# Turned keys placed four copies to a block in the next unit's feed-forward, and unit 7's keys turned on VectorE too

## The chip, the cores and the metric

The kernel runs on one core of a Trainium2 chip. The core has five engines that run side by side, each from its own queue in order: TensorE (matrix products; PE in the profile, PEld for its weight loads), VectorE (DVE), ScalarE (ACT), GpSimd (POOL) and SyncE (SP, which here only issues DMA transfers). The metric is the time of one execution in microseconds (us); the runs of one kernel are told by their median.

## The reference

Two parts follow each other. The first is a linear attention with a complex decay, for 4 batches, 8 heads, 768 tokens and a head width of 48; the second a feed-forward layer on its output, without a nonlinearity between the two products.

```python
scale = np.minimum(mag, 0.999) / (mag + 1e-06)          # mag = |a_re + i a_im|
for t in range(S):                                      # S = 768, D = 48
    S_re, S_im = ar * S_re - ai * S_im + kv, ar * S_im + ai * S_re
    y[:, :, t] = np.einsum('bhd,bhde->bhe', q[:, :, t], S_re)
x = y.transpose(0, 2, 1, 3).reshape(B * S, H * D)       # 3072 x 384
return (x @ w_a) * (x @ w_b) @ w_out                    # d_ff = 1536
```

## The kernel before

**Units.** The work is cut into 12 units (`NU`): two pairs of batches, and for each pair six chunks of 128 tokens of all heads. A unit is 256 tokens of the feed-forward. Within a chunk the recurrence is written as matrix products: decays are multiplied up along the chunk (*preparation*, `prep`), queries and keys are scaled by them, and then come scores, outputs and the update of the carried state (*attention*, `attn`).

**Stages.** The main loop runs over `w`, the unit whose feed-forward is worked. I call one turn of it stage w. It has 12 blocks `f`, one for each 128 of the 1536 hidden columns. In a block TensorE makes the first product (`gemm1`, L546, 18 products into a PSUM bank `ab`, of which there are three), and then the second product (`gemm2`, L567, 6 products into the two output banks `o`) of the block two before (`LAG = 2`), so the last two second products of a unit run in blocks 0 and 1 of the next stage. Then the output banks are evicted by two copies on ScalarE (L706) before block 2's second product, the first of the new unit, may write them; there is one pair of banks.

Behind each first product stands a chain: ScalarE copies half the bank (L557, into `h_t` or, in odd blocks, into a buffer `o_sb`), VectorE multiplies by the other half (L558), ScalarE rounds to `hh` (L559), VectorE makes the rest `hl` (L560). The second product reads `hh` and `hl`.

**Attention between the blocks.** In stage w the attention of unit w+1 is laid piece by piece between the products: scores (L429, masked by VectorE into `am`, L432), transposes of the keys, outputs (L473), rest of the outputs, state (L496, which reads the turned keys `kt`). `ATTN_AT` or `LATE_ATTN_AT` says in which block it begins; it is over by block 10 or 11 (`STACK_AT`). The preparation of unit w+2 also runs on VectorE and ScalarE in stage w and the end of the one before; its results go out as ten or so transfers `stk<-qk` on SyncE (`stack`, L366).

**Turning the keys.** The state product needs the keys with tokens on the partitions. Up to unit 7 (`KT_FROM = 8`) TensorE turns them: 16 transposes for a unit (L440), evicted by four copies on ScalarE (L443). From unit 8 on `turn_keys` turns 32x32 blocks on VectorE (four instructions, L396) into the unit's own decay tile `a_t`, and `place_keys` puts the blocks in their place in `kt` with 16 copies on ScalarE (L406). There is one buffer `kt`. These 16 copies are issued in one go in block 10 of the stage before the one whose attention reads them. A unit without a next chunk (5 and 11) needs no turned keys.

What hangs on `KT_FROM` besides: in a unit turned on VectorE the two products of queries and keys with the decays (L319, 1536 elements wide) are cut into four of 768, attention begins in block 4 (`LATE_ATTN_AT`) and has 13 pieces for 16; and the load of the decay tile of unit u+2 is put off, since the turned keys lie in the old one (`apool` has two buffers). `late_decays` (units from `KT_FROM + 2`) says that a unit's decay scaling (`scale`, five passes on VectorE and seven on ScalarE) is made at the start of its own preparation and not within the one before.

**Order.** A scheduler orders each engine's instructions by priority and by dependences, after costs of its own; `tc.high_priority` lifts the chain behind the first product and the attention's evictions, and `tc.issue_after(x)` keeps an instruction behind x on the queue. `ff_last[0]` is the last matrix product of the feed-forward.

Of the kernel before, what the change touches and what calls it, by code (L numbers as in the profile page):

```python
# [22 lines left out]
NU = NBP * NCH  # L23
# [22 lines left out]
LAG = 2  # L46
HB = 3
OWN_FROM = 2
KT_FROM = 8
GATE_FROM = 2  # L50
O_BUFS = 3
CONV_ON_AB = 7
# [20 lines left out]
def tile_kernel(ctx: ExitStack, tc: tile.TileContext, a_d, qk_d, v_d, w_d, qn_d, kn_d, vn_d, an_d, out_d):  # L73
    nc = tc.nc
    vec, act, pe, sync = nc.vector, nc.scalar, nc.tensor, nc.sync
# [48 lines left out]
    def r(ap):  # L124
        return ap.bitcast(F32R)
# [34 lines left out]
    def load_a(u):  # L160
        t = apool.tile([128, 2, W], F32, name="a_t")
        for hs in halves if u == 0 else (slice(0, W),):
            sync.dma_start(out=t[:, :, hs], in_=a_d[u, :, :, hs])
        return t

    a_tiles = {}
# [38 lines left out]
    def late_decays(u):  # L205
        return u >= KT_FROM + 2 and (u - 1) % NCH

    def prep(u):
# [129 lines left out]
        yield 1000  # L338
        if u < KT_FROM or c + 1 == NCH:
            for k in range(2):  # L340
# [14 lines left out]
    def load_qk(u):  # L355
        sync.dma_start(out=qk[:, :, 1, 0:2 * TOK], in_=qk_d[u])

    def stack(u):
        n = RUN if rescaled(u % NCH) else 2 * TOK
        for h in range(H):  # L360
            r0 = h * D
            while r0 < (h + 1) * D:
                j, p = divmod(r0, 128)
                m = min((h + 1) * D - r0, 128 - p)
                d0 = 2 * (r0 - h * D)
                sync.dma_start(out=stk[d0:d0 + 2 * m, h, 0:n], in_=qk[p:p + m, j, :, 0:n])  # L366
                r0 += m
# [4 lines left out]
    def load_v(u):  # L372
        for i in range(2):
            t = vpool.tile([128, VW], F32, name="v_t")
            for c0, s0, n in ((0, 0, 64), (64, 80, 48)):
                sync.dma_start(out=t.rearrange("p (g e) -> p g e", g=H // 2)[:, :, c0:c0 + n],
                               in_=v_d[u, i].rearrange("p (g e) -> p g e", g=H // 2)[:, :, s0:s0 + n])
            v_tiles[u, i] = t
# [9 lines left out]
    kt_pending = {}  # L388

    def new_kt(u):  # L390
        kt_tiles[u] = kvp.tile([128, 2, H * KS], F32, name="kt", bufs=1)
# [8 lines left out]
    def place_keys(u, t):  # L400
        new_kt(u)
        src = t.rearrange("p s w -> p (s w)").rearrange("p (t g x) -> p t g x", t=4, g=G)
        dst = kt_tiles[u].rearrange("p i (j b x) -> p (i j) b x", j=NJ, b=4)
        for tb in range(4):
            for pb in range(4):
                act.copy(out=dst[tb * 32:(tb + 1) * 32, :, pb], in_=src[pb * 32:(pb + 1) * 32, tb])  # L406

    ff_last = [None]

    def attn(u, xh, xl):  # L410

# [2 lines left out]
        ams, xps = {}, {}  # L414
        if not last and u < KT_FROM:
            new_kt(u)
# [71 lines left out]
        def state(i, hg):  # L488
# [12 lines left out]
            with tc.high_priority(offset=ATTN_FIRST):  # L501
# [4 lines left out]
                if rescaled(c):  # L506
# [5 lines left out]
                 (state, 1, 0), (residual, 1, 0), (state, 1, 1)]  # L512
        if u >= KT_FROM:
            order = [(scores, 0, 0), (scores, 0, 1), (pause, 0, 0), (outputs, 0, 0), (scores, 1, 0),
# [7 lines left out]
        for fn, i, g in order:  # L522
            if not (last and fn is state or fn is transposes and (last or u >= KT_FROM)):
                fn(i, g)
                yield

    def pieces(u):
        if u >= KT_FROM:
            return 9 if u % NCH + 1 == NCH else 13
        return 8 if u % NCH + 1 == NCH else 16  # L530

    def new_x():
        return (moe.tile([128, NJ, TOK], F32, name="xh"), moe.tile([128, NJ, TOK], F32, name="xl"))


    def w_ab(f, part, blk):
        m, b = divmod(blk, NJ)
        return w_t[f, m][:, part, b * 128:(b + 1) * 128]

    def gemm1(f, xh, xl, ps_ab=ps_ab, moe=moe, spare=None):  # L540
        ab = ps_ab.tile([128, 512], F32, name="ab")
        for m in range(2):
            n = 0
            for i in range(NJ):
                for part, xt in ((0, xh), (0, xl), (1, xh)):
                    ff_last[0] = pe.matmul(out=ab[:, m * TOK:(m + 1) * TOK],  # L546
                              lhsT=r(w_ab(f, part, m * NJ + i)),
                              rhs=r(xt[:, i, :]), start=n == 0, stop=n == 8).ins
                    n += 1
        if spare and f % 2:  # L550
            h_t = spare()[:, 0:TOK]
        else:
            h_t = moe.tile([128, TOK], F32, name="h_t", bufs=1)
        hh = moe.tile([128, TOK], F32, name="hh", bufs=HB)
        hl = moe.tile([128, TOK], F32, name="hl", bufs=HB)
        with tc.high_priority(offset=MOE_FIRST):
            act.copy(out=h_t, in_=ab[:, 0:TOK])  # L557
            vec.tensor_tensor(out=h_t, in0=ab[:, TOK:2 * TOK], in1=h_t, op=ALU.mult)  # L558
            act.copy(out=r(hh), in_=h_t)  # L559
            vec.tensor_tensor(out=r(hl), in0=h_t, in1=hh, op=ALU.subtract)  # L560
        return hh, hl

# [113 lines left out]
    def drain(gen, ns=None):  # L676
        if gen is None:
            return
        left = ns
        for cost in gen:  # L680
            if left is not None:
                left -= cost or 0
                if left <= 0:
                    return
# [14 lines left out]
    def second():  # L699
        w2, f2, hh, hl, os2 = pend.pop(0)  # L700
        gemm2(f2, hh, hl, os2)
        if f2 == NF - 1:
            for tt in range(2):
                o_sb = moe.tile([128, DM], F32, name="o_sb", bufs=O_BUFS)
                with tc.high_priority(offset=MOE_FIRST):
                    act.copy(out=o_sb, in_=os2[tt][:, 0:DM])  # L706
                act.dma_start(out=out_d[w2, tt], in_=o_sb)

    def spare_h(w, f):
        if w > 0:  # L710
            return lambda: moe.tile([128, DM], F32, name="o_sb", bufs=O_BUFS)
        if f <= ATTN_AT[0]:
            return lambda: kvp.tile([128, 2, H * KS], F32, name="kt", bufs=1)[:, 0]

    def attn_at(w):
        return LATE_ATTN_AT if w + 1 >= KT_FROM else ATTN_AT[min(w, 4)]

    pgen = None
    for w in range(NU):
        last = w + 1 == NU  # L720
        x_nxt = None if last else new_x()
        at = None if last else attn(w + 1, *x_nxt)
        if not last:
            load_v(w + 1)
        os_ = [ps_o.tile([128, 512], F32, name=f"o{t}") for t in range(2)]
        slots = [0, 2 * (STACK_AT[min(w, 4)] + 1 - max(attn_at(w), 0 if w else P1_AT + 1))]
        left = [pieces(w + 1)]

        def slot():
            if at is None or f < attn_at(w) or (w == 0 and f <= P1_AT) or not slots[1]:  # L730
                return
            n = -(-left[0] // slots[1])
            slots[1] -= 1
            for _ in range(n):
                next(at, None)
                left[0] -= 1

        for f in range(NF):
            if w == 0:
                next(ws, None)  # L740
                drain(p1, P1_F)
                if f == P1_AT:
                    drain(p1)
                    stack(1)
                    load_qk(2)
                    pgen = prep(2)
            pend.append((w, f, *gemm1(f, *x_cur, spare=spare_h(w, f)), os_))
            slot()
            if len(pend) > LAG:
                second()  # L750
            slot()
            if f == STACK_AT[min(w, 4)]:
                drain(at)
                if w + 2 < NU:
                    drain(pgen)
                    if w + 2 in kt_pending:
                        place_keys(w + 2, kt_pending.pop(w + 2))
                    stack(w + 2)
                if w + 3 < NU:
                    load_qk(w + 3)  # L760
                    pgen = prep(w + 3)
                if w + 4 < NU and w + 4 not in a_tiles:
                    a_tiles[w + 4] = load_a(w + 4)
            if w > 0:
                drain(pgen, 2400)
        x_cur = x_nxt
# [74 lines left out]
```

## Time and profile before

| | |
|---|---|
| median of 3 runs | 689.01 us (688.86 to 690.12) |
| profiled execution | 689.64 us, of which 687.9 is the span of the instructions |
| TensorE busy (PE) | 642.6 us, 93% |
| VectorE busy (DVE) | 555.0 us, 81% |
| ScalarE busy (ACT) | 329.1 us, 48% |
| L440, transposes of keys on TensorE | x112, 255 ns mean |
| L406, copies that place turned keys | x48, 511 ns mean |
| L706, evictions of the output banks | x22, 481 ns mean |

Times of a row are counted from the start of the span. A matrix product's duration contains the filling and draining of the array, so that of products in a row the distance from start to start is what each costs. Starts of the stages (first L546 product): stage 5 at 343.11, 6 at 393.11, 7 at 444.09, 8 at 493.25, 9 at 543.94, 10 at 594.51.

### The profile page before, as it was taken

The page shows a single profiled execution, that of the slowest core. Times are in us where ns is not written, and L with a number is a line of the kernel's source. Part 1 is how long each engine was busy: PE and PEld are TensorE (multiplying, and loading weights), DVE is VectorE, ACT ScalarE, POOL GpSimd, SP SyncE. Part 2 cuts the span into 40 slices and gives each one's busy share as a digit, 9 for nine tenths or more (in the row PEclk, how much of TensorE's full clock was granted, in tenths as well). Part 3 has the DMA queues.
Part 4 walks back from the last instruction along what each step waited for, and adds up shares of the span by engine and source line. Part 5 has one row for each costly group of instructions (what it writes and reads, how often), then busy time and mean ns, then how long its engine had stood idle before and what let it go on. Part 6 is the DMA issues. An engine that isn't in the chain of part 4 may idle for free.

```text
span 687.9 us, 14250 instructions
## 1 busy us (share of the span) xinstructions
PE 642.6 (93%) x5794; PEld 605.8 (88%) x5794; DVE 555.0 (81%) x1277; ACT 329.1 (48%) x658; POOL 5.5 (1%) x11
## 2 busy tenths in 40 slices
PE   3547899999999999999999999999999999999996
PEld 1224789999999999999999999999989989999996
DVE  5999999998989989989899899898898588432221
ACT  6347665634545446264363554555735733222221
POOL 3000000000000000000000000000000000000000
PEclk9566999999999999999999999999999999999998
DMA  8983300512415215042160340530520500400000
GB/s 286 390 312 92 118 2 7 181 51 65 122 39 150 60 51 171 16 131 92 27 192 17 108 127 2 126 109 11 157 70 18 150 24 15 106 24 2 24 1 28
DMA packets 52120, 63.14 MB, mean 92 GB/s; under 512 B 28624, under 2 KB 32208, under 8 KB 52048
## 3 DMA queue, kind: packets, MB, share of 16 engines
q1 hardware_dynamic: 48592, 57.45, 28.0%
q10 hardware_dynamic: 3456, 4.72, 1.9%
q8 instruction: 47, 0.77, 0.5%
q14 instruction: 25, 0.20, 0.1%
HBM read 38.54 MB, written 4.72 MB: 63 GB/s over the span
## 4 chain that ended last, share of the span: by engine, by line
PE 57%; DVE 26%; ACT 7%; DMA 6%; issue 2%; SPq 1%; DVEq 0%; ACTq 0%
PE ab L546 28%; PE o L567 14%; DMA w<-in_dram 5%; PE xp L473 4%; PE pm L429 4%; PE pm L496 3%; DVE a_t L299 3%; DVE qk L319 2%; ACT kt L406 2%; DVE hl L560 2%; DVE pr L237 2%; DVE z L304 1%; PE pm L440 1%; DVE am L432 1%; DVE h_t L558 1%
## 5 line engine op out<-in xcount | busy, mean ns | idle before, releaser
L546 PE MATMUL ab<-xh,w 128*128 128x256 f32 x1728 | 339.4, 285 | 0.0
L546 PEld LDWEIGHTS ab<-xh,w 128*128 128x128 f32 x1728 | 276.2, 189 | 2.4 <-issue 1.6
L546 PE MATMUL ab<-xl,w 128*128 128x256 f32 x864 | 244.3, 283 | 0.0
L546 PEld LDWEIGHTS ab<-xl,w 128*128 128x128 f32 x864 | 162.8, 188 | 0.5
L567 PE MATMUL o<-w,hh 128*128 128x384 f32 x576 | 154.0, 346 | 2.8 <-ACT o_sb L706 2.8
L567 PEld LDWEIGHTS o<-w,hh 128*128 128x128 f32 x576 | 97.1, 188 | 5.2 <-ACT o_sb L706 4.1
L567 PE MATMUL o<-w,hl 128*128 128x384 f32 x288 | 97.3, 338 | 0.0
L557 ACT COPY h_t<-ab 128x256 f32<-128x256 f32 x75 | 27.7, 370 | 72.0 <-PE ab L546 68.9
L152 PE MATMUL ab<-o_sb,ident 128*128 128x384 f32 x42 | 29.2, 794 | 30.4 <-DVE o_sb L143 30.4
L558 DVE TENSOR_TENSOR h_t<-ab,h_t 128x256 f32<-128x256 f32 x75 | 31.5, 420 | 30.7 <-ACT h_t L557 30.7
L429 PE MATMUL pm<-stk 128*128 128x128 f32 x384 | 54.8, 282 | 0.6 <-DMA stk<-qk 0.5
L429 PEld LDWEIGHTS pm<-stk 128*128 128x128 f32 x384 | 50.3, 195 | 4.7 <-issue 3.2
L567 PEld LDWEIGHTS o<-w,hl 128*128 128x128 f32 x288 | 54.1, 188 | 0.0
L557 ACT COPY o_sb<-ab 128x256 f32<-128x256 f32 x66 | 24.3, 368 | 60.5 <-PE ab L546 60.2
L559 ACT CAST hh<-h_t 128x256 fp32r<-128x256 f32 x75 | 30.1, 402 | 47.5 <-DVE h_t L558 47.3
L558 DVE TENSOR_TENSOR o_sb<-ab,o_sb 128x256 f32<-128x256 f32 x66 | 27.6, 419 | 29.0 <-ACT o_sb L557 29.0
L237 DVE TENSOR_TENSOR pr<-z 128x384 f32<-128x384 f32 (+1 forms) x91 | 47.2, 524 | 2.4 <-ACT z L223 0.3
L559 ACT CAST hh<-o_sb 128x256 fp32r<-128x256 f32 x66 | 26.6, 404 | 46.4 <-DVE o_sb L558 46.3
L152 PEld LDWEIGHTS ab<-o_sb,ident 128*128 128x128 f32 x42 | 10.2, 286 | 40.0 <-DVE o_sb L143 29.4
L299 DVE TENSOR_TENSOR a_t<-z,b_t 128x768 f32<-128x768 f32 x48 | 44.6, 951 | 0.0
L319 DVE TENSOR_TENSOR qk<-qk,z 128x768 f32<-128x768 f32 (+1 forms) x32 | 43.2, 1349 | 0.2
L560 DVE TENSOR_TENSOR hl<-h_t,hh 128x256 fp32r<-128x256 f32 x75 | 31.4, 419 | 10.5 <-ACT hh L559 10.5
(117 smaller groups left out, 898.4 us busy)
## 6 DMA issues: line engine op xcount, KB each, us to landing
w<-in_dram SPq DMA_DIRECT2D x36, 384.0 KB, 7.9
qk<-in_dram SPq DMA_DIRECT2D x12, 768.0 KB, 4.9
stk<-qk SPq DMA_DIRECT2D x48, 192.0 KB, 3.3
a_t<-in_dram SPq DMA_DIRECT2D x11, 768.0 KB, 4.3
stk<-qk SPq DMA_DIRECT2D x24, 192.8 KB, 3.4
out_dram<-o_sb ACTq DMA_DIRECT2D x24, 192.0 KB, 1.9
v_t<-in_dram SPq DMA_DIRECT2D x24, 128.0 KB, 2.7
v_t<-in_dram SPq DMA_DIRECT2D x24, 96.0 KB, 3.0
```

The lines of the kernel that those rows point to most:

```text
L152: pe.matmul(out=lp[:, 0:n], lhsT=ident, rhs=t, start=True, stop=False)
L237: vec.tensor_tensor(out=pr[:, :, :, o:o + n], in0=view(zz, W + at_(i) + 2 * o, [[W, 2], [-W, 2], [2, n]]), in1=tok(slice(1, 3), i - 1, o, ...
L299: vec.tensor_tensor(out=pz[:, s].rearrange("p (j b e) -> p j b e", j=SUB // 2, e=2), in0=zb[:, 1 + s], in1=view(bb, (1 + k - s) * NB, [[0, ...
L319: vec.tensor_tensor(out=qk4[:, :, k, x0:x1], in0=qk4[:, :, 1, x0:x1], in1=z[:, k].rearrange("p (j t) -> p j t", j=NJ).unsqueeze(2).broadca ...
L429: pe.matmul(out=sp[:, h4], lhsT=stk[:, h, ks], rhs=stk[:, h, qs], start=True, stop=True)
L473: run = pe.matmul(out=xp[qd * 32:(qd + 1) * 32, ti], lhsT=l, rhs=rr, start=st, stop=sp_, tile_position=(0, qd * 32), skip_group_check=True ...
L546: ff_last[0] = pe.matmul(out=ab[:, m * TOK:(m + 1) * TOK], lhsT=r(w_ab(f, part, m * NJ + i)), rhs=r(xt[:, i, :]), start=n == 0, stop=n == ...
L557: act.copy(out=h_t, in_=ab[:, 0:TOK])
L558: vec.tensor_tensor(out=h_t, in0=ab[:, TOK:2 * TOK], in1=h_t, op=ALU.mult)
L559: act.copy(out=r(hh), in_=h_t)
L560: vec.tensor_tensor(out=r(hl), in0=h_t, in1=hh, op=ALU.subtract)
L567: ff_last[0] = pe.matmul(out=os_[tt][:, 0:DM], lhsT=r(ht[:, ts]), rhs=r(w_t[f, 2][:, part, :]), start=(f == 0 and n == 0), stop=(f == NF - ...
```

## The change

Unit 7 is turned on VectorE as well (`KT_FROM = 7`). The 16 copies are no longer issued together in block 10 of the stage before; they are issued in the stage that works the unit's attention, four in each of blocks 1 to 4, each four behind the rounding `hh` of their block (`ff_last[1]`). The load of the decay tile that waits for these copies is issued in block 5.

```diff
-KT_FROM = 8
+KT_FROM = 7
+PLACE_AT = 1
...
         for tb in range(4):
-            for pb in range(4):
-                act.copy(out=dst[tb * 32:(tb + 1) * 32, :, pb], in_=src[pb * 32:(pb + 1) * 32, tb])
-
-    ff_last = [None]
+            with tc.issue_after(ff_last[1]):
+                for pb in range(4):
+                    act.copy(out=dst[tb * 32:(tb + 1) * 32, :, pb], in_=src[pb * 32:(pb + 1) * 32, tb])
+            yield
+
+    ff_last = [None, None]
...
-            act.copy(out=r(hh), in_=h_t)
+            ff_last[1] = act.copy(out=r(hh), in_=h_t).ins
...
-    pgen = None
+    pgen, placing = None, iter(())
...
                     drain(pgen)
-                    if w + 2 in kt_pending:
-                        place_keys(w + 2, kt_pending.pop(w + 2))
                     stack(w + 2)
...
-                if w + 4 < NU and w + 4 not in a_tiles:
-                    a_tiles[w + 4] = load_a(w + 4)
+            if f == PLACE_AT and w + 1 in kt_pending:
+                placing = place_keys(w + 1, kt_pending.pop(w + 1))
+            next(placing, None)
+            if f == PLACE_AT + 4 and w + 3 < NU and w + 3 not in a_tiles:
+                a_tiles[w + 3] = load_a(w + 3)
```

**The order that comes of it.** Line numbers of the changed kernel are one to four higher (L709 is L706 of before, L562 is L559, L560 is L557, L408 is L406, L224 is L223, L432 is L429, L549 is L546, L570 is L567). ScalarE, end of stage 8 and start of stage 9; `kt` is the placed keys of unit 10, the two `o_` tiles are the output banks of stage 8. Before:

```order
L406 COPY kt<-a_t 32x6x64 x5
L557 COPY h_t<-ab 128x256
L406 COPY kt<-a_t 32x6x64 x2
L559 CAST hh<-h_t 128x256
L223 ACTIVATE z<-z 128x768
L557 COPY o_sb<-ab 128x256
L706 COPY o_sb<-o_6127 128x384
L707 DMA out_dram<-o_sb 128x384
L559 CAST hh<-o_sb 128x256
L706 COPY o_sb<-o_6128 128x384
```

and now:

```order
L224 ACTIVATE z<-z 128x768
L560 COPY o_sb<-ab 128x256
L709 COPY o_sb<-o_6106 128x384
L562 CAST hh<-o_sb 128x256
L709 COPY o_sb<-o_6107 128x384
L710 DMA out_dram<-o_sb 128x384 x2
L408 COPY kt<-a_t 32x6x64 x2
L560 COPY h_t<-ab 128x256
L408 COPY kt<-a_t 32x6x64 x2
L562 CAST hh<-h_t 128x256
L408 COPY kt<-a_t 32x6x64 x4
L560 COPY o_sb<-ab 128x256
```

The key copies have moved from ahead of the two evictions to behind them, and the second eviction still stands behind the `hh` of block 1.

VectorE, end of unit 7's preparation (stage 5): `z` and `a_t` are its decays, `qk` its queries and keys. Before:

```order
L304 TENSOR_TENSOR z<-a_t 128x768
L558 TENSOR_TENSOR h_t<-ab,h_t 128x256
L432 TENSOR_TENSOR am<-pm,mask 128x512
L313 TENSOR_TENSOR a_t<-a_t 128x768
L560 TENSOR_TENSOR hl<-h_t,hh 128x256
L328 TENSOR_TENSOR a_t<-a_t 128x768
```

and now, up to the same row and then at the preparation's very end:

```order
L305 TENSOR_TENSOR z<-a_t 128x768
L320 TENSOR_TENSOR qk<-qk,z 128x3x256
L561 TENSOR_TENSOR h_t<-ab,h_t 128x256
L435 TENSOR_TENSOR am<-pm,mask 128x512
L563 TENSOR_TENSOR hl<-h_t,hh 128x256
L314 TENSOR_TENSOR a_t<-a_t 128x768
L320 TENSOR_TENSOR qk<-qk,z 128x3x256
L329 TENSOR_TENSOR a_t<-a_t 128x768
```

```order
L335 TENSOR_TENSOR qk<-qk,a_t 128x3x256
L320 TENSOR_TENSOR qk<-qk,z 128x3x256
L561 TENSOR_TENSOR h_t<-ab,h_t 128x256
L320 TENSOR_TENSOR qk<-qk,z 128x3x256
L563 TENSOR_TENSOR hl<-h_t,hh 128x256
L397 STREAM_TRANSPOSE a_t<-qk 128x4x96 x4
```

Two of the four half-wide products stand ahead of L329 now, and the four turns behind the last one.

TensorE, middle of stage 6. Before, the transposes of unit 7's first half lay within the first product of block 7 (`stk` holds its queries and keys, `w_816` the weights):

```order
L429 MATMUL pm<-stk 128x128 x8
L567 MATMUL o_4816<-w_478,hh 128x384 x2
L567 MATMUL o_4816<-w_478,hl 128x384
L567 MATMUL o_4817<-w_478,hh 128x384 x2
L567 MATMUL o_4817<-w_478,hl 128x384
L546 MATMUL ab<-xh,w_816 128x256
L440 MATMUL pm<-ident,stk 128x96 x4
L546 MATMUL ab<-xl,w_816 128x256
L546 MATMUL ab<-xh,w_816 128x256
L440 MATMUL pm<-ident,stk 128x96 x4
```

and now, where unit 7's first scores come, two blocks earlier:

```order
L549 MATMUL ab<-xh,w_468 128x256
L432 MATMUL pm<-stk 128x128 x4
L570 MATMUL o_4854<-w_418,hh 128x384 x2
L570 MATMUL o_4854<-w_418,hl 128x384
L570 MATMUL o_4855<-w_418,hh 128x384 x2
L570 MATMUL o_4855<-w_418,hl 128x384
L432 MATMUL pm<-stk 128x128 x4
L549 MATMUL ab<-xh,w_488 128x256
```

No transposes of unit 7 are left on TensorE; its two scores are a second product apart.

## The prediction

> **What bounds the kernel now.** I read the slices of the span first, to see which engine is full where; then busy time by stage, to find stages whose length is not TensorE's work; then TensorE's waits, and the timeline of ScalarE around the longest of them.
>
> The slices (the span in 40 parts of 17.2 us, tenths busy):
>
> ```profile
> PE   3547899999999999999999999999999999999996
> PEld 1224789999999999999999999999989989999996
> DVE  5999999998989989989899899898898588432221
> ACT  6347665634545446264363554555735733222221
> ```
>
> TensorE is full from the seventh slice on, VectorE nearly so up to the 33rd, ScalarE half. What shortens TensorE's stages shortens the run; VectorE has little room before stage 9.
>
> Busy time by stage: length, then PE, PEld, DVE, ACT and POOL. The rows are stages 5 to 9; a stage begins with its first L546 matmul.
>
> ```profile
> core 0 of [0], span 687.9 us
> 343.11:393.11 50.00, 49.23 (x434) 47.88 (x434) 45.77 (x98) 24.81 (x51) 0.00 (x0) 1.00 0.34 98
> 393.11:444.09 50.98, 50.57 (x497) 49.56 (x497) 48.65 (x110) 25.74 (x50) 0.00 (x0) 1.00 0.33 90
> 444.09:493.25 49.16, 49.16 (x482) 48.00 (x481) 42.17 (x98) 28.29 (x57) 0.00 (x0) 1.00 0.32 89
> 493.25:543.94 50.69, 49.50 (x481) 48.02 (x481) 44.62 (x101) 29.18 (x58) 0.00 (x0) 1.00 0.28 79
> 543.94:594.51 50.57, 49.28 (x481) 48.05 (x481) 36.87 (x88) 20.20 (x44) 0.00 (x0) 1.00 0.21 59
> ```
>
> Stages 7, 8 and 9 carry the same matrix work (attention of units 8, 9, 10, keys turned on VectorE). Stage 7 has no idle time, 8 and 9 have 50.69 - 49.50 = 1.19 and 50.57 - 49.28 = 1.29 us. Stage 6 still turns keys on TensorE and is 1.82 us longer than stage 7, 0.41 of it idle. The granted clock is 1.00 in all five. Who kept TensorE waiting between 400 and 600 us (total, times, longest):
>
> ```profile
> PE o L567 <- ACT o_sb L706: 2.4, 3, 1.3
> PE pm L440 <- DVE am L432: 0.4, 1, 0.4
> ```
>
> Three waits, all for the eviction of the two output banks; none for hh or a free ab bank. ScalarE before the longest one, at the start of stage 9, and TensorE beside it:
>
> ```profile
> 549.15 0.37 ACT L557 COPY h_t<-ab 128x256 f32<-128x256 f32 x1
> 549.55 1.03 ACT L406 COPY kt<-a_t 32x384 f32<-32x384 f32 x2
> 550.61 0.41 ACT L559 CAST hh<-h_t 128x256 fp32r<-128x256 f32 x1
> 550.92 0.84 ACT L223 ACTIVATE z<-z 128x768 f32<-128x768 f32 x1
> 551.66 0.35 ACT L557 COPY o_sb<-ab 128x256 f32<-128x256 f32 x1
> 551.92 0.49 ACT L706 COPY o_sb<-o 128x384 f32<-128x384 f32 x1
> 552.43 0.34 ACTq L707 DMA_DIRECT2D out_dram<-o_sb  x1
> 553.71 0.41 ACT L559 CAST hh<-o_sb 128x256 fp32r<-128x256 f32 x1 [1.30 <-DVE o_sb L558]
> 554.02 0.47 ACT L706 COPY o_sb<-o 128x384 f32<-128x384 f32 x1
> ```
>
> ```profile
> 549.29 0.52 PE L567 MATMUL o<-w,hh 128*128 128x384 f32 x2
> ...
> 554.54 0.63 PE L567 MATMUL o<-w,hh 128*128 128x384 f32 x2 [1.29 <-ACT o_sb L706]
> ```
>
> Block 1's first product was complete at 549.29. ScalarE copied it out at 551.66, 2.4 us late, because the last key copies and an ACTIVATE that they had held up stood ahead. So VectorE's product was late, the cast hh waited 1.30 us for it, and the second eviction, queued behind hh, came at 554.02; TensorE lost 1.29 us.
>
> **The change, part by part.**
>
> *The burst is spread (units 8, 9, 10).* The same 16 copies now stand behind both evictions, four to a block in blocks 1 to 4, so block 1 finds ScalarE on time. The second eviction keeps its place behind hh. Taking away 2.4 us of lateness is more than the 1.29 us lost; I take both idle times as gone and stages 8 and 9 at stage 7's length: 1.53 + 1.41 = 2.94 us. The bounds: nothing (VectorE's product is late by itself) and these 2.94. Stage 7 had a burst too, with the third, smallest wait; what it may give (0.2) I leave to pay for new short waits.
>
> *What hides the copies.*
>
> ```profile
> L406 ACT COPY kt<-a_t x48: 493/511/515, 441.1 to 550.1; 32x384 f32<-32x384 f32 x48
> L443 ACT COPY kt<-pm x28: 462/480/487, 76.1 to 431.2; 128x384 f32<-128x384 f32 x28
> ```
>
> ```profile
> 444.25 2.15 PE ab L546 x18
> 446.41 1.05 PE o L567 x6
> 447.46 2.15 PE ab L546 x18
> ```
>
> A block without attention takes 447.46 - 444.25 = 3.21 us on TensorE. ScalarE then has 4 x 0.511 + 0.37 + 0.41 = 2.82 us per block: it fits, with 0.4 to spare. If that cover failed, each of 16 such blocks (four stages) could cost up to 4 x 0.511. But second products follow their first by two blocks, 6.4 us, and the burst, denser than this, made no wait for hh. I take 0. The copies are ready well before block 7, where the state product first reads them; their new wait, behind hh, is on their own engine.
>
> *Unit 7 off TensorE.* Two groups of eight transposes go; one of them on TensorE, and what follows it:
>
> ```profile
> 430.33 0.82 PE L440 MATMUL pm<-ident,stk 96*128 96x96 f32 x8
> 430.93 0.36 PE L546 MATMUL ab<-xh,w 128*128 128x256 f32 x1
> ```
>
> Eight take 0.60 us, sixteen 1.20; the idle 0.41 in stage 6 was a wait of exactly these transposes for VectorE's am. With 0.2, which I put to changing over twice, that is the 1.82 us by which stage 6 exceeds stage 7. I take 1.82; bounds 1.2 and 1.8, less what follows. ScalarE gives up four copies of 0.48 and gains sixteen of 0.511, 6.3 us, in a stage where it works 25.74 of 50.98.
>
> *VectorE's added work.*
>
> ```profile
> L319 DVE TENSOR_TENSOR qk<-qk,z x32: 936/1352/1759, 46.3 to 584.5; 128x768 f32<-128x768 f32 x16, 128x1536 f32<-128x1536 f32 x16
> L334 DVE TENSOR_TENSOR qk<-qk,a_t x12: 946/949/955, 55.6 to 581.2; 128x768 f32<-128x768 f32 x12
> L396 DVE STREAM_TRANSPOSE a_t<-qk x12: 528/544/574, 433.0 to 528.0; 128x384 f32<-128x384 f32 x12
> ```
>
> ```profile
> 383.41 0.96 DVE L328 TENSOR_TENSOR a_t<-a_t 128x768 f32<-128x768 f32 x1 [2.42 <-ACT a_t L315]
> ```
>
> Unit 7's preparation, in stage 5, gains four turns, 4 x 0.544 = 2.2 us, and splits two products of 1.76 into four of 0.94, +0.2. Two of the four move ahead of L328, where VectorE sat idle 2.42 us, and fill 1.9 of it. So the last product ends about 1 us earlier than now, and the turns put what follows about 1 us later. The nearest reader is the hh ahead of stage 6's second eviction; 1 us late is less than the 2.4 - 1.29 = 1.1 us that stage 9 bore without loss. I take 0 and keep 2.4 as the bound.
>
> *Unit 9's decay scaling moves* from unit 8's preparation to the start of its own: five VectorE passes leave stage 6 and enter stage 7.
>
> ```profile
> L184 DVE SCALAR_TENSOR_TENSOR a_t<-a_t x9: 949/951/952, 58.9 to 395.7; 128x768 f32<-128x768 f32 x9
> ```
>
> 5 x 0.951 = 4.75 us: stage 6 falls to about 44 busy, stage 7 rises to about 47 of 49.2. Unit 10 already works so in stages 7 and 8. I take 0; bound 4.75.
>
> *Unit 7's attention starts in block 4, not 6* (the rule for units turned on VectorE). SyncE's queue now, and unit 8's first scores:
>
> ```profile
> 391.34 7.33 SPq L366 DMA_DIRECT2D stk<-qk  x10
> 401.29 0.60 SPq L356 DMA_DIRECT2D qk<-in_dram  x1
> ```
>
> ```profile
> 459.27 1.05 PE L429 MATMUL pm<-stk 128*128 128x128 f32 x8
> ```
>
> Unit 8's scores come 459.27 - 444.09 = 15.2 us into stage 7; unit 7's will come at 393.11 + 15.2 = 408.3. Their operands have landed at 401.29, when the load that overwrites their source goes out: 7 us to spare. Costs 0. The load of unit 9's decays now goes behind these ten transfers, after unit 7's key copies (about 410), where two value loads and, far later, unit 8's transfers are behind it; even at 10 us it lands by 420, and its first reader comes after unit 8's preparation, near 434. Costs 0.
>
> The sum: 687.9 - 2.94 - 1.82 = 683.1 of span; with the 1.7 us outside it the profiled execution of 689.64 becomes 684.9. The median of the runs, 689.01, lies 0.6 below that execution: **684.2 us**.
>
> **A rule weighed.** The Trainium skill ("VectorE: DVE Perf Modes", Rules for kernel authors) gives a 128x128 transpose to TensorE when PSUM will do as its destination, and VectorE's only within 32x32 blocks. Counted by engine time this trace agrees: 1.2 us of TensorE and 1.9 of ScalarE become 2.2 and 8.2 elsewhere. By that rule unit 7's part would lose; its time is the second rival's.
>
> **Rivals.**
>
> 1. *The eviction stays late.* Its place behind hh is unchanged, and in the fence above hh waited for VectorE, not for a key copy. Then stages 8 and 9 keep 2.94: 689.0 - 1.8 = 687.2. Against it: ScalarE was 2.4 us late before VectorE could begin. It decides where VectorE by itself holds the product over 1.1 us. Chance 0.13.
> 2. *VectorE pays for unit 7.* With VectorE at 45.77 of 50.00 and 48.65 of 50.98, the 2.4 us go to TensorE as waits and the 1.82 are not gained: 689.0 - 2.94 + 2.4 = 688.5. Against it: the idle 2.42, and the 4.75 that leave stage 6. Chance 0.06.
> 3. *Slower: the spread copies hold up hh.* In stages 6 to 9 sixteen blocks carry four copies each; if the chain behind a first product had no room, each block would pay a copy, 16 x 0.51 = 8.2: 689.0 - 4.8 + 8.2 = 692.4. It passes the old time at 0.3 us per block. Against it: no wait for hh now, behind up to five copies in a row. Chance 0.05.
>
> **How the numbers follow.** The forecast has 0.73 (its own range 683.0 to 685.9: the bounds of unit 7's part, plus short waits). The rivals have 0.13, 0.06 and 0.05; 0.03 is left for gains beyond 683.0. 0.2% is 1.4 us, about what timing can tell from no change. Faster than 687.6: the forecast, rival 1 and the gains beyond, 0.87 after two hundredths off for a mixture; same: rival 2 and that mixture, 0.08; slower: 0.05. The range, 682.8 to 687.3, takes in the first rival and leaves out the others.
>
> **What would show it.** Right: stages 6 to 9 of 49.2 us or less, no wait of L567 for the evictions over 0.3 us there, L440 gone from stage 6, no wait for hh. Wrong: evictions still a microsecond late (rival 1); waits for am, or for stk before 408, in stages 5 and 6 (rival 2); waits for hh or a late L557 in blocks 2 to 5 (rival 3).

## The result

| | before | changed |
|---|---|---|
| median | 688.96 us (688.34 to 690.12, 6 runs) | 683.21 us (682.98 to 683.51, 6 runs) |
| profiled execution, span | 689.64, 687.9 us | 683.28, 681.5 us |
| PE busy | 642.6 us, 93% | 639.5 us, 94% |
| DVE busy | 555.0 us, 81% | 558.1 us, 82% |
| ACT busy | 329.1 us, 48% | 334.9 us, 49% |

The ratio of the times is 0.9915 [0.9902, 0.9928]: 5.75 us less. Predicted were 684.2 (682.8 to 687.3).

Two of the slices' rows after the change, to be read against the first fence of the prediction:

```profile
PEld 1214789999999999999999999999999999999996
DVE  6999899998989989989899899899899898433221
```

The two slices of PEld that stood at eight in the last third are nine tenths or more now. VectorE, which had a dip to five in the 32nd slice, stays at eight or nine tenths up to the 34th. Busy time by stage, stages 5 to 9, each from its first L549 product (length, then the busy time of PE, PEld, DVE and ACT):

```profile
341.64:391.59 49.95, 49.21 (x433) 47.90 (x433) 47.22 (x103) 24.42 (x50) 0.00 (x0) 1.00 0.30 84
391.59:440.56 48.97, 48.97 (x482) 48.07 (x482) 44.13 (x101) 29.09 (x56) 0.00 (x0) 1.00 0.42 117
440.56:489.69 49.13, 49.04 (x481) 48.07 (x481) 42.69 (x100) 29.09 (x58) 0.00 (x0) 1.00 0.26 77
489.69:538.64 48.95, 48.95 (x481) 48.05 (x481) 44.97 (x103) 28.07 (x56) 0.00 (x0) 1.00 0.28 81
538.64:588.12 49.48, 49.24 (x482) 48.09 (x482) 42.05 (x94) 23.42 (x49) 0.00 (x0) 1.00 0.20 55
```

Stage 6 went from 50.98 to 48.97, stage 8 from 50.69 to 48.95, stage 9 from 50.57 to 49.48; stages 5 and 7 stayed. Stages 6 to 9 together: 201.40 to 196.53, 4.87 us less. Stages 6 and 8 have no idle time at all now. Of the signs that the prediction named, one failed: stage 9, at 49.48, is longer than 49.2. Who kept TensorE waiting between 390 and 600 us is one row where it was three waits for evictions and one for a mask:

```profile
PE xp L476 <- DVE am L435: 0.2, 1, 0.2
```

ScalarE at the start of stage 9, where the copy out of `ab` had come 2.4 us late, and TensorE beside it:

```profile
544.68 0.85 ACT L224 ACTIVATE z<-z 128x768 f32<-128x768 f32 x1 [0.46 <-DVE z L222]
545.43 0.35 ACT L560 COPY o_sb<-ab 128x256 f32<-128x256 f32 x1
545.69 0.48 ACT L709 COPY o_sb<-o 128x384 f32<-128x384 f32 x1
546.28 0.41 ACT L562 CAST hh<-o_sb 128x256 fp32r<-128x256 f32 x1
...
546.59 0.47 ACT L709 COPY o_sb<-o 128x384 f32<-128x384 f32 x1
...
547.47 1.04 ACT L408 COPY kt<-a_t 32x384 f32<-32x384 f32 x2 [0.41 <-ACT o_sb L709]
```

```profile
544.00 0.52 PE L570 MATMUL o<-w,hh 128*128 128x384 f32 x2
...
547.20 0.52 PE L570 MATMUL o<-w,hh 128*128 128x384 f32 x2
```

The copy out of `ab` comes at 545.43, 1.4 us after block 1's first product was complete (544.00); before it came 2.4 us after. The order is the same, `hh` first and then the second eviction, but `hh` waits for nothing, and block 2's second product follows after 3.20 us, a block's own length. So 1.4 us of lateness is borne; the prediction had worked out 1.1 for it.

### The profile page after: what moved, and what is told of

Its sections match the earlier page's. It is cut to its first block, busy times and chain, and to the rows that moved or that the text cites. A ratio compares the mean times of both kernels' runs of the same rounds, so it can differ in the third digit from the quotient of the medians.

```text
span 681.5 us, 14237 instructions
## 1 busy us (share of the span) xinstructions
PE 639.5 (94%) x5778; PEld 603.5 (89%) x5778; DVE 558.1 (82%) x1283; ACT 334.9 (49%) x670; POOL 5.5 (1%) x11
## 4 chain that ended last, share of the span: by engine, by line
PE 53%; DVE 32%; ACT 7%; DMA 3%; issue 3%; SPq 2%; ACTq 0%; DVEq 0%
PE ab L549 27%; PE o L570 13%; PE xp L476 4%; PE pm L432 4%; DVE a_t L300 3%; PE pm L499 3%; DVE qk L320 3%; DVE pr L238 2%; DVE hl L563 2%; DVE am L435 2%; ACT kt L408 2%; DVE z L305 1%; DVE o_sb L142 1%; DVE h_t L561 1%; DVE z L244 1%
## 5 line engine op out<-in xcount | busy, mean ns | idle before, releaser
L549 PE MATMUL ab<-xh,w 128*128 128x256 f32 x1728 | 339.2, 285 | 0.0
L549 PEld LDWEIGHTS ab<-xh,w 128*128 128x128 f32 x1728 | 276.1, 188 | 2.8 <-issue 2.0
L549 PE MATMUL ab<-xl,w 128*128 128x256 f32 x864 | 244.3, 283 | 0.0
L549 PEld LDWEIGHTS ab<-xl,w 128*128 128x128 f32 x864 | 162.8, 188 | 0.5
L570 PE MATMUL o<-w,hh 128*128 128x384 f32 x576 | 153.7, 346 | 0.4 <-ACT o_sb L709 0.4
L570 PEld LDWEIGHTS o<-w,hh 128*128 128x128 f32 x576 | 97.3, 188 | 1.5 <-ACT o_sb L709 0.6
L570 PE MATMUL o<-w,hl 128*128 128x384 f32 x288 | 97.3, 338 | 0.0
L560 ACT COPY h_t<-ab 128x256 f32<-128x256 f32 x75 | 27.6, 368 | 67.5 <-PE ab L549 65.4
L432 PE MATMUL pm<-stk 128*128 128x128 f32 x384 | 54.6, 281 | 0.6 <-DMA stk<-qk 0.5
L570 PEld LDWEIGHTS o<-w,hl 128*128 128x128 f32 x288 | 54.1, 188 | 0.0
L432 PEld LDWEIGHTS pm<-stk 128*128 128x128 f32 x384 | 50.1, 194 | 4.4 <-issue 2.2
L560 ACT COPY o_sb<-ab 128x256 f32<-128x256 f32 x66 | 24.3, 369 | 59.7 <-PE ab L549 59.1
L562 ACT CAST hh<-h_t 128x256 fp32r<-128x256 f32 x75 | 30.1, 402 | 44.2 <-DVE h_t L561 44.1
L562 ACT CAST hh<-o_sb 128x256 fp32r<-128x256 f32 x66 | 26.6, 403 | 45.1 <-DVE o_sb L561 44.9
L300 DVE TENSOR_TENSOR a_t<-z,b_t 128x768 f32<-128x768 f32 x48 | 45.1, 954 | 0.0
L476 PE MATMUL xp<-am,v_t 128*32 128x128 f32 x768 | 37.7, 281 | 2.9 <-DVE am L435 2.8
```

The source lines that it names most:

```text
L300: vec.tensor_tensor(out=pz[:, s].rearrange("p (j b e) -> p j b e", j=SUB // 2, e=2), in0=zb[:, 1 + s], in1=view(bb, (1 + k - s) * NB, [[0, ...
L432: pe.matmul(out=sp[:, h4], lhsT=stk[:, h, ks], rhs=stk[:, h, qs], start=True, stop=True)
L476: run = pe.matmul(out=xp[qd * 32:(qd + 1) * 32, ti], lhsT=l, rhs=rr, start=st, stop=sp_, tile_position=(0, qd * 32), skip_group_check=True ...
L549: ff_last[0] = pe.matmul(out=ab[:, m * TOK:(m + 1) * TOK], lhsT=r(w_ab(f, part, m * NJ + i)), rhs=r(xt[:, i, :]), start=n == 0, stop=n == ...
L562: ff_last[1] = act.copy(out=r(hh), in_=h_t).ins
L570: ff_last[0] = pe.matmul(out=os_[tt][:, 0:DM], lhsT=r(ht[:, ts]), rhs=r(w_t[f, 2][:, part, :]), start=(f == 0 and n == 0), stop=(f == NF - ...
```

## The experiments

All are against the kernel before on the same chip; the ratio's interval tells whether it differs. Stage lengths in the table are of the profiled executions, each from the first product to the next stage's (hundredths can differ from the fences by rounding). A clean stage with turned keys will turn out to be 48.95 us.

| us | 5 | 6 | 7 | 8 | 9 | 10 | median |
|---|---|---|---|---|---|---|---|
| before | 49.99 | 50.99 | 49.16 | 50.69 | 50.57 | 46.14 | 688.92 to 689.34 |
| changed | 49.95 | 48.96 | 49.14 | 48.95 | 49.47 | 46.14 | 683.21 |
| changed, again | 50.02 | 48.93 | 48.95 | 48.95 | 49.42 | 46.14 | 683.16 |
| spread alone | 49.98 | 51.01 | 49.22 | 49.83 | 49.00 | 46.14 | 687.1 |
| unit 7 alone | 50.01 | 49.83 | 50.81 | 49.45 | 52.63 | 47.96 | 692.54 |
| eviction first | 49.93 | 50.91 | 49.22 | 50.65 | 50.42 | 46.14 | 689.09 |
| one go, behind | 49.96 | 48.97 | 49.55 | 49.61 | 49.79 | 46.14 | 686.08 |
| copies twice | 50.01 | 50.38 | 52.25 | 51.26 | 51.06 | 46.14 | 693.15 |
| turns four times | 50.00 | 48.93 | 48.95 | 53.94 | 53.99 | 49.17 | 697.22 |
| unit 6 too | 47.60 | 49.12 | 49.57 | 49.62 | 51.51 | 48.27 | 688.2 |
| blocks 0 to 3 | 49.98 | 48.93 | 49.12 | 49.15 | 50.31 | 46.14 | 684.96 |
| blocks 2 to 5 | 49.99 | 48.93 | 48.95 | 48.95 | 48.95 | 46.14 | 682.72 |
| mask first | 50.06 | 48.93 | 48.95 | 48.95 | 48.95 | 46.14 | 683.22 |
| masks and evictions first | 49.76 | 48.93 | 49.10 | 48.95 | 49.01 | 46.14 | 683.42 |

**The changed kernel again.** No edit.

> The changed kernel once more, beside the kernel before on the same chip, since the runs of the last four spread by 2 us and the first ones by half. Theory (stages 6 to 9 carry 4.9 us; the rest of the measured 5.75 is in the start of the run and moves from run to run): ratio 0.9915 to 0.993, with stages 6 to 9 within 0.1 us of those of its first trace. Rival (the start is faster by the change): the first stage begins over 0.7 us earlier in both profiles.

683.16 us, ratio 0.9918 [0.9905, 0.9931], before 689.19: the gain is there again. Stages 6, 8 and 9 repeat to 0.05 us, stage 7 does not: it is 0.19 shorter than in the first trace, so a tenth or two in a single stage says little. The first stage begins at 77.76 us, against 76.81 in the first trace and 78.50 in the kernel before: 0.74 earlier than before, so the rival isn't excluded (more on this at the end).

**The spreading alone** (changed kernel, unit 7 on TensorE).

```diff
-KT_FROM = 7
+KT_FROM = 8
```

> The spread alone: unit 7's keys stay on TensorE, the copies of units 8, 9 and 10 stand four to a block behind the evictions. Theory (two causes that add: evictions held up by the burst, 2.8 us in stages 8 and 9; transposes and their wait, 2.0 us in stage 6): stages 8 and 9 at 49.0 to 49.5, stage 6 still at 51.0, time about 689.0 - 2.8 = 686.2. Rival (the two parts need each other, or the start of the run carries part of the gain): under 685.3 or over 687.5.

687.1 us, ratio 0.9974 [0.9965, 0.9983]: 1.8 us gained. The evictions' waits are gone from stages 8 and 9. What is left of stage 8 is a wait for the mask; of TensorE's waits between 390 and 600 us the longest row, and VectorE there:

```profile
PE xp L476 <- DVE am L435: 1.0, 2, 0.8
```

```profile
512.25 0.72 DVE L435 TENSOR_TENSOR am<-pm,mask 128x512 f32<-128x512 f32 x1
512.85 0.99 DVE L320 TENSOR_TENSOR qk<-qk,z 128x768 f32<-128x768 f32 x1
513.72 0.72 DVE L435 TENSOR_TENSOR am<-pm,mask 128x512 f32<-128x512 f32 x1
```

The wait is new, most of it in stage 8: the second mask (513.72) stands behind a product of the preparation, and the attention's outputs wait for it. So the spreading does what it says to the evictions (stages 8 and 9 together 2.43 of the 2.94), and lets a mask come late where an eviction had. Stage 8 had been expected at 49.0 to 49.5 and the median at 686.2.

**Unit 7 alone** (kernel before, with the burst).

```diff
-KT_FROM = 8
+KT_FROM = 7
```

> Unit 7 alone: turned on VectorE, but its 16 copies in one burst in block 10 of stage 5, as those of the other units still are. Theory: stage 6 loses its transposes and the wait for am (2.0 us) but gets an eviction wait like those of stages 8 and 9 (1.2 to 1.5 us) at its start; stages 8 and 9 stay at 50.6; time 688.2 to 689.0. Rival (VectorE pays for the turns): over 689.0, with waits for am or stk in stages 5 and 6. Rival (a burst costs only where VectorE has more to do): 687.0.

692.54 us, ratio 1.0053 [1.0039, 1.0066]: 3.6 us slower. The two parts do not add up: apart they give -1.8 and +3.6, together -5.75. TensorE's two longest rows of waits from 390 to 640 us; ScalarE from the end of stage 5 on; VectorE's pass of unit 8's preparation that follows the ACTIVATE of L223, here and in the changed kernel; VectorE's waits for `hh` from 390 to 600, here and in the changed kernel; and the transfers of the first and last of units 8 to 11:

```profile
PE pm L429 <- DMA stk<-qk: 3.4, 2, 2.0
PE o L567 <- ACT o_sb L706: 2.0, 3, 1.3
```

```profile
393.51 2.08 ACT L406 COPY kt<-a_t 32x384 f32<-32x384 f32 x4
...
404.39 0.51 ACT L406 COPY kt<-a_t 32x384 f32<-32x384 f32 x1
404.92 0.84 ACT L223 ACTIVATE z<-z 128x768 f32<-128x768 f32 x1
```

```profile
405.80 0.56 DVE L237 TENSOR_TENSOR pr<-z 128x384 f32<-128x384 f32 x1 [1.88 <-ACT z L223]
```

```profile
393.14 0.55 DVE L238 TENSOR_TENSOR pr<-z 128x384 f32<-128x384 f32 x1
```

```profile
DVE hl L560 <- ACT hh L559: 14.1, 16, 1.3
```

```profile
DVE hl L563 <- ACT hh L562: 4.2, 11, 0.6
```

```profile
441.03 6.69 SPq L366 DMA_DIRECT2D stk<-qk  x10
...
622.89 6.74 SPq L366 DMA_DIRECT2D stk<-qk  x10
```

With a burst each stage from 5 on, all 16 copies stand ahead of the first ACTIVATE of the next preparation (L223), as in the prediction's fence of the start of stage 9, and between the copies and casts of several blocks. So unit 8's preparation goes on behind this ACTIVATE only 11.7 us into stage 6 (405.80 less 394.10), in the changed kernel 1.6 us into it (393.14 less 391.59). In the kernel before only the last of its three bursts ended ahead of that ACTIVATE; the first two began behind it (441.09 behind 437.28, 490.94 behind 490.18). VectorE waited for ScalarE's `hh` 14.1 us, in the changed kernel 4.2. The transfers of the four units go out at 441.03, 502.75, 564.25 and 622.89; in the changed kernel they do at 428.24, 480.19, 530.16 and 582.28, so the transfers are 13, 23, 34 and 41 us later (1.4 of it from a later start of that execution, and from unit 9 on also what the stages themselves have lost), until the scores wait for `stk` in stages 9 and 10. The changed kernel differs from this one only in when the copies, and the load behind them, are issued. The load goes out earlier here than there (404.92, 10.8 us into stage 6, for 411.76, 20.2 us into it), so it isn't the load: it is the burst that makes unit 7 costly.

**The eviction ahead of `hh`** (kernel before, the burst kept).

```diff
-                with tc.high_priority(offset=MOE_FIRST):
+                with tc.high_priority(offset=MOE_FIRST + 40000):
                     act.copy(out=o_sb, in_=os2[tt][:, 0:DM])
```

> The kernel before with one edit: the copies that evict the output banks get a higher priority, so that the second stands ahead of hh of block 1 on ScalarE's queue; the burst stays ahead of both. Theory (the wait is ScalarE's lateness plus the wait of hh for VectorE that the second eviction inherits): without the 1.3 us of hh in between, both evictions come within about 1.3 us of the late copy, just in time; stages 8 and 9 at 49.2 to 49.6, time 686.2 to 687.0. Rival (lateness behind the burst alone holds the evictions): stages 8 and 9 keep over 0.8 us of wait each, time over 688.

689.09 us, ratio 1.0004 [0.9994, 1.0014]: no change. ScalarE at the start of stage 9:

```profile
551.54 0.35 ACT L557 COPY o_sb<-ab 128x256 f32<-128x256 f32 x1
551.79 0.48 ACT L706 COPY o_sb<-o 128x384 f32<-128x384 f32 x1
...
552.68 0.48 ACT L706 COPY o_sb<-o 128x384 f32<-128x384 f32 x1 [0.41 <-PE ab L546]
553.58 0.41 ACT L559 CAST hh<-o_sb 128x256 fp32r<-128x256 f32 x1 [0.42 <-DVE o_sb L558]
```

Here the copy of `ab` is as late as before (551.54), yet the second eviction comes at 552.68 for 554.02, ahead of `hh`, and TensorE's wait of 1.29 us for it is gone. So both are needed for that wait: ScalarE late, and the place behind `hh`. Stage 9 gained only 0.15 all the same, and not the microsecond that was expected. TensorE's waits from 390 to 600 us:

```profile
PE o L567 <- ACT o_sb L706: 1.1, 2, 0.8
PE xp L473 <- DVE am L432: 0.8, 1, 0.8
```

The first row is of stage 8 (at 502 and 504), where the scheduler left the order as it was, so that stage tells nothing of the place; the second is new, a mask at 565 in stage 9.

**The copies behind both evictions, but in one go** (changed kernel; all 16 issued in block 1).

```diff
             with tc.issue_after(ff_last[1]):
...
-            yield
+        yield
```

> The changed kernel with all 16 copies issued at once in block 1 behind its hh, not four to a block. Theory (it counts that the copies stand behind the evictions, and blocks 1 to 4 have room on ScalarE): no new wait, 683.0 to 683.6. Rival (four to a block is what keeps hh on time): waits for hh or for a late copy out of ab in blocks 2 to 4, over 684.0.

686.08 us, ratio 0.996 [0.9947, 0.9974]: half of the gain. Stage 6 keeps all of its part; stages 7 to 9 lose 1.4 against the changed kernel, in waits for masks. All of TensorE's waits from 390 to 600 us, and VectorE ahead of the first of them, at 464:

```profile
PE xp L476 <- DVE am L435: 1.8, 3, 0.6
```

```profile
462.33 0.42 DVE L563 TENSOR_TENSOR hl<-h_t,hh 128x256 fp32r<-128x256 f32 x1 [0.45 <-ACT hh L562]
...
462.87 0.95 DVE L300 TENSOR_TENSOR a_t<-z,b_t 128x768 f32<-128x768 f32 x1
463.74 0.68 DVE L435 TENSOR_TENSOR am<-pm,mask 128x512 f32<-128x512 f32 x1
```

The run of copies ends at 461.86, right ahead of ScalarE's `hh` (461.89); VectorE's `hl` waits for it, and what is queued behind, a pass of the preparation (L300) and the mask, comes late. TensorE does not wait for `hh` or `hl`, which it reads two blocks later, but for the mask. What does not come back is the lateness of the burst in block 10: the transfers of unit 8 go out 12.2 us ahead of stage 7, as in the changed kernel (12.3).

```profile
430.52 7.96 SPq L367 DMA_DIRECT2D stk<-qk  x10
```

So for the preparation it is enough that the copies stand behind its first passes; that they are spread is worth the 1.4 us of mask waits.

**Each copy made twice** (changed kernel).

```diff
-                for pb in range(4):
+                for pb in (0, 0, 1, 1, 2, 2, 3, 3):
```

> The changed kernel with each of the 16 copies made twice, so eight to a block: 8 x 0.51 + 0.78 = 4.9 us of ScalarE in a block of 3.2 us. Theory (the copies are free as long as they fit beside TensorE, 2.82 of 3.21): blocks 1 to 4 of stages 6 to 9 put ScalarE 4 x 1.7 = 6.7 us behind, past the room of the chain; waits for am, hh or a bank of ab of 1 to 4 us in a stage, time 687 to 697. Rival (two blocks of room hide even that): within 0.5 us of the changed kernel.

693.15 us, ratio 1.0065 [1.0052, 1.0078], 10 us more than the changed kernel. TensorE's two longest rows of waits from 390 to 600 us:

```profile
PE xp L476 <- DVE am L435: 3.9, 5, 1.3
PE pm L432 <- DVE am L435: 2.2, 3, 1.0
```

So ScalarE's cover ends between 2.82 us per block and 2.82 + 2.04 = 4.86, where a block has 3.21. What TensorE waits for is the mask again, and not `hh` (it waits 0.5 us for the copies themselves). It is VectorE that waits for `hh`, 8.0 us for 4.2 in the changed kernel:

```profile
DVE hl L563 <- ACT hh L562: 8.0, 18, 0.7
```

**Each turn made four times** (changed kernel; 12 more turns, 6.5 us, in each unit on VectorE).

```diff
-            for i in range(2):
+            for i in (0, 0, 0, 0, 1, 1, 1, 1):
```

> The changed kernel with each turn on VectorE made four times: 12 x 0.54 = 6.5 us more of VectorE for each of units 7 to 10. Theory (the 2.4 us of unit 7 were free because VectorE had an idle 2.4 us and about 1 us of room behind it, and units 8 to 10 have 4 to 7 us of room in their stages): stage 6 gets waits of 2 to 5 us at its start, stages 7 to 9 lose under 1 us each, time 685.5 to 690. Rival (VectorE pays for every turn): 4 x 6.5 = 26 us more. Rival (VectorE has room throughout): within 0.5 us of the changed kernel.

697.22 us, ratio 1.0129 [1.0112, 1.0145]. Neither the theory nor a rival came true: stages 6 and 7 are untouched, stages 8, 9 and 10 lose 5.0, 4.5 and 3.0. Stage 9 is the only one from 5 to 10, in all these traces, with a granted clock under 1.00: 0.97, lowered from about 591 to 597 us, right behind its longest wait (2.3 us, to 590.96). TensorE's busy time there is 50.60 for 49.24, so 1.4 of the 4.5 us are not waits. TensorE's waits from 490 to 650 us, and the transfers of units 9 and 11:

```profile
PE pm L432 <- DMA stk<-qk: 4.3, 6, 1.4
PE pm L499 <- ACT kt L408: 3.9, 2, 2.3
```

```profile
501.31 7.72 SPq L367 DMA_DIRECT2D stk<-qk  x10
...
629.58 6.69 SPq L367 DMA_DIRECT2D stk<-qk  x10
```

These and unit 10's (564.34) are 21, 47 and 34 us later than in the changed kernel, 1.2 of it from a later start; those of unit 8, at 438.90, were 11 us later without a wait. VectorE's lead over TensorE is a stock: each unit draws on it, and nothing waits until it is used up. Two runs bound how large it is, counted from the start of the stage that reads the transfers. Unit 9's went out 8.0 us into stage 8 with unit 7 alone, and nothing waited for them; here they go out 10.2 us into it (501.31 less 491.11), and the scores wait. In the changed kernel they go out 9.5 us ahead of that stage, so for unit 9 its stock lies between 17.5 and 19.7 us.

**Unit 6 on VectorE too** (changed kernel).

```diff
-KT_FROM = 7
+KT_FROM = 6
```

> The changed kernel with unit 6 turned on VectorE too. Unit 6 is a first chunk: its attention lies in stage 5, which has a wait of 0.55 us for am before its transposes. Theory (TensorE gives up 1.2 to 1.4 us of transposes and that wait; VectorE, with 45.8 of 50.0 us busy in stage 5 before, takes 2.4 us more and unit 8's scaling moves on): stage 5 from 49.95 to 48.0 to 49.0, time 1 to 2 us under the changed kernel. Rival (VectorE is full there): waits for stk or late evictions in stages 5 and 6 that take it back, at or over the changed kernel.

688.2 us, ratio 0.9985 [0.9973, 0.9997]. Stage 5 falls to 47.60, 2.35 less, as stage 6 fell for unit 7; stages 6 to 10 give back 0.2, 0.4, 0.7, 2.0 and 2.1, with these two rows as the longest of TensorE's waits from 390 to 650 us:

```profile
PE pm L432 <- DMA stk<-qk: 2.7, 3, 1.9
PE o L570 <- ACT o_sb L709: 0.9, 3, 0.4
```

One more unit than the stock allows: the gain comes in stage 5, most of the bill in stages 9 and 10. The first waits for `stk` are of unit 10, whose transfers go out 11.8 us into stage 9.

**Where the copies are placed** (changed kernel; blocks 0 to 3, and 2 to 5).

```diff
-PLACE_AT = 1
+PLACE_AT = 0
```

```diff
-PLACE_AT = 1
+PLACE_AT = 2
```

> The changed kernel with the copies one block earlier, four in each of blocks 0 to 3, so that four to six stand ahead of the two evictions. Theory (evictions are late when ScalarE is late at block 1; four copies and the chain are 2.82 of 3.21 us in block 0, so it is not): 683.0 to 684.0, no wait for the evictions over 0.4 us. Rival (any copies ahead of the evictions hold them up): an eviction wait of 0.5 to 1.5 us in each of stages 6 to 9, 685 to 688.

> The changed kernel with the copies one block later, in blocks 2 to 5, beside the first scores and masks of the next unit. Theory (the copies fit beside a block; what they can delay is the mask am, which stands on VectorE behind hl, which waits for hh): waits for am of 0.2 to 0.8 us in stages 6 to 9, 683.2 to 685.0. Rival (the place within the stage is free): within 0.2 us of the changed kernel.

From block 0: 684.96 us, ratio 0.9942 [0.9927, 0.9957]; no wait for an eviction over 0.4 us, but mask waits of 0.1 in stages 7 and 8 and of 1.0 in stage 9, which neither the theory nor the rival had. From block 2: 682.72 us, ratio 0.9901 [0.9885, 0.9917], and no wait at all between 390 and 600, where waits for the mask were expected. Its stages 6 and 9:

```profile
393.55:442.48 48.93, 48.93 (x481) 48.03 (x481) 44.07 (x101) 28.97 (x56) 0.00 (x0) 1.00 0.42 115
...
540.38:589.33 48.95, 48.95 (x482) 48.05 (x481) 41.09 (x93) 23.27 (x49) 0.00 (x0) 1.00 0.22 63
```

They are all matrix work, as are 7 and 8; the four take 0.75 us less than in the changed kernel's first trace and 0.47 less than in its second. This has the lowest median, clearly below the kernel before; against the changed kernel (683.16 to 683.21) the difference lies within the intervals.

**Masks first** (changed kernel: the product that makes `am`), **and masks and evictions** (changed kernel: all that is lifted with `ATTN_FIRST`, and the evictions as above).

```diff
-            with tc.high_priority(offset=ATTN_FIRST):
+            with tc.high_priority(offset=MOE_FIRST + 2000):
```

```diff
-ATTN_FIRST = 2000
+ATTN_FIRST = 6000
```

> The changed kernel with the mask am ahead of the feed-forward's chain in VectorE's priorities. Theory (the waits for am, 0.5 us at 366 and 0.3 to 0.5 in stages 6 to 9, come from the order on VectorE alone): they go, time 682.2 to 683.0. Rival (am waits for what stands ahead anyway, and hl behind it comes later): 683.0 to 684.5.

> The changed kernel with all high priorities of the attention, and the evictions of the output banks, ahead of the feed-forward's chain. Theory: as for the mask alone, and the eviction wait of 0.5 us at 350 goes too; 681.5 to 682.8. Rival (the chain pays: hh and hl late): over 683.5.

683.22 us, ratio 0.9914 [0.9898, 0.9931], and 683.42, ratio 0.9914 [0.99, 0.9928]. The first takes the last mask wait out of stage 9 (48.95; stage 7 was clean in the changed kernel's second trace without it) and leaves the one of 0.4 us in stage 5. The second takes out the eviction wait of stage 5 (49.76). Both medians lie above the times that the theories gave. In the medians neither differs from the changed kernel: what they take away is under 0.8 us of stages, less than these medians resolve.

## Why the prediction was right, and where its terms were off

**The burst.** Predicted 2.94 us for stages 8 and 9, measured 1.74 + 1.10 = 2.84. Stage 8 gave 0.2 more than its term because stage 7, taken as the length without waits, still held its own small one: a clean stage is 48.95 and not 49.16. (The prediction put the third wait of its fence into stage 7; the three lie at 502.25 and 503.89, in stage 8, and at 554.54. Stage 7's lateness is 0.2 us at 453, spread over products that count as busy.) Stage 9 gave 0.3 less, as a mask wait took part of the eviction's place. That the two so nearly cancel, and that the mask waits are as small as 0.2 us, where the spreading alone has 1.0, is luck: the sum sets 0.2 us aside for new short waits and does not ask where they would come from. Rival 1, that the eviction stays late because of its place behind `hh`, is refuted by the fence of stage 9 after: same place, no wait. But the place was half of the cause, as the eviction put ahead of `hh` shows. The Trainium skill ("Perfetto Trace Analysis", Per-engine timelines) says that ScalarE's and VectorE's queues are strictly first in, first out; the traces agree: before, the second eviction, at 554.02, stood behind an `hh` that waited 1.30 us, while the last product into its bank had started at 550.17.

**Unit 7 off TensorE.** Predicted 1.82, measured 2.02: the whole of stage 6's excess over a clean stage, 0.2 more for the reason just given. No transposes are left there, and the wait of 0.41 for the mask went with them. The 1.20 of transposes and that wait leave 0.4; that this is changing over, as the prediction has it of 0.2, no run shows.

**VectorE's 2.4 us at no cost.** Held for TensorE. VectorE at the end of unit 7's preparation:

```profile
382.04 0.96 DVE L329 TENSOR_TENSOR a_t<-a_t 128x768 f32<-128x768 f32 x1 [1.35 <-ACT a_t L316]
...
387.59 0.95 DVE L320 TENSOR_TENSOR qk<-qk,z 128x768 f32<-128x768 f32 x1
...
388.80 1.95 DVE L397 STREAM_TRANSPOSE a_t<-qk 128x384 f32<-128x384 f32 x4
```

The product that had waited 2.42 us for ScalarE now waits 1.35, since two of the half-wide ones went ahead of it. The last product ends at 388.5, 46.9 us into the stage, and the turns take 1.95 for the 2.2 that were worked out. The transfers follow, and have landed at 399.76, when the next load goes out, against 406.58 for unit 7's first scores:

```profile
389.20 7.91 SPq L367 DMA_DIRECT2D stk<-qk  x10
...
399.76 0.58 SPq L357 DMA_DIRECT2D qk<-in_dram  x1
```

```profile
406.58 1.05 PE L432 MATMUL pm<-stk 128*128 128x128 f32 x8
```

The reason given, the idle time and the 1 us of room ahead, was too local: the turns, and what moves with them, are paid out of the lead. The transfers of units 9, 10 and 11 go out 9.5, 8.5 and 5.8 us ahead of their stages, for 12.3, 12.3 and 8.2 before. Nor did unit 9's decay scaling enter stage 7, as the prediction had it: it starts at 430.20, still in stage 6, and VectorE's busy time in stage 7 is 42.69 and not about 47. That term's cost of nothing held, its reason did not. Rival 2 is what happens one unit further, or with 6.5 us more per unit, and its wait does not come in the same stage: it comes where the stock is used up. The rule of the Trainium skill that was weighed ("VectorE: DVE Perf Modes", Rules for kernel authors) thus loses here for unit 7 and would have been the better guide for unit 6, by the 5.0 us that unit 6 costs against the changed kernel.

**The copies hidden.** Held, at 2.82 of 3.21 us per block; doubled they cost 10 us. Rival 3 had the right resource and the wrong waiter: when ScalarE is late, TensorE does not wait for `hh` but for the mask that stands on VectorE's queue behind `hl`.

**The parts taken one by one.** This step failed, without harm to the sum: the prediction priced the two parts as if each stood by itself. Unit 7 with the burst loses 3.6 us. Only where the copies stand behind the evictions and the preparation's first passes does ScalarE leave VectorE the room that unit 7 draws on; in one go there they still give half of the gain. The spreading does without unit 7: alone it gives 2.3 us in stages 6 to 9.

**The sum.** Predicted 4.76 us, measured 4.87 in stages 6 to 9 of the profiled executions, 5.75 in the medians. In the first pair of traces no other stage differs by more than 0.1 us; what differs is when the first stage begins, at 78.5 us before, at 76.8 in the first trace of after and at 77.8 in the second, though the medians are the same. The interval of the second comparison (4.8 to 6.5 us) takes in 4.87, that of the first (5.0 to 6.8) just does not. A trace is of one execution, and the second one's took 685.13 us, 2.0 over its median; so the traces don't tell whether the change makes the start earlier, and what the 0.9 us is stays open.

## What to carry to other kernels

Of an engine that works ahead of the bound one, ask how far ahead it is and what each unit draws from that lead, not only whether the next reader is on time: a move that gains at once can be paid for several stages later. A run of copies on an in-order engine is best issued in pieces behind what others wait for, since it delays less its own reader than whatever stands second in the queue of the next engine. And two edits that share an engine are to be priced together: here one of them costs 3.6 us without the other and saves 2.0 us of its stage with it.

## What the runs showed that was not expected

- A late ScalarE shows up on TensorE as a wait for a mask that VectorE makes, by way of `hl`: 3.9 + 2.2 us of such waits with copies made twice, and none for `hh`.
- 6.5 us of added work per unit on VectorE made the transfers of units 8 to 11 late by 11, 21, 34 and 47 us. Counted from the start of the stage that reads them it is 9, 20, 28 and 36 us, 8 to 11 for each unit and so more than the 6.5 added. Why more stays open.
- Sixteen copies of half a microsecond, issued in one go ahead of the next unit's preparation, made its transfers 13 us late (unit 7 with the burst), on an engine that is half idle; in one go behind its first passes they did not.
